# A two-branch attention kernel on one core: another order of the units, the last output rows in halves, the first weights in column halves

## The chip, the core and the metric

The kernel runs on one core of a Trainium2 chip. A core has a matrix engine (TensorE, PE in the profile), a vector engine (VectorE, DVE), a scalar engine (ScalarE, ACT), a general engine (GpSimd, POOL) and a queue engine (SyncE, SP) that here issues every DMA. Each engine runs its own instructions in order and waits on semaphores for the others. Matmuls write to eight banks of an accumulation memory (PSUM); ACT and DVE copy results out of it ("evacuate" it). The metric is the device time of one execution in microseconds (us), the median of the runs.

## The reference, cut to what matters

Two branches read the same x of 2048 rows by 512 and are mixed row by row with a gate. Everything is bf16.

```python
# branch A: 64 segments of 32 rows, 32 heads of 128, one after the other
mem = mem0                                   # 8 rows
for s in range(64):
    h = concat([mem, x[32*s : 32*s + 32]])   # 40 rows
    q, k, v = h @ Wq, h @ Wk, h @ Wv         # 512 -> 32 x 128 each
    p = softmax(where(mask, q @ k.T * scale, -1e9))
    o = (p @ v) @ Wo
    mem = o[:8]                              # the next segment reads it
    outs.append(o[8:])
# branch B: 4 blocks of 512 rows, 32 heads of 16
for s in range(4):
    a_dot = softmax(qs @ ks.T * scale + causal) @ vs
    a_mem = (phi(qs) @ M) / (phi(qs) @ z + 1e-6)      # M, z sum phi(k).T @ v over earlier blocks
    o_B = sigmoid(beta) * a_mem + (1 - sigmoid(beta)) * a_dot
b = concat(o_B) @ wo
g = sigmoid((x * gate_w).sum(-1))
out = g * a + (1 - g) * b
```

Segment s+1 of branch A needs the 8 memory rows that segment s puts out, so the segments form a chain. Branch B is free of it and fills gaps.

## The kernel before

**First phase (to about 50 us).** x, branch B's weights and then branch A's weights (4 MB each for Wk, Wq, Wv) are loaded. x is turned by TensorE (`x_chunk`, L588), and `b_projections` works out K, Q and V of branch B for three of the four blocks. `pk` (L686) multiplies one quarter f (128 of the 512 columns) of wk or wq with a block's x; its result is evacuated to `stgk[f]` and stored to DRAM (`scr_kqd`). `pv` (L704) does the same for V, `mz` (L738) for the memory matrix `MZ` (stored to `scr_mzd`). `plan_loads` issues the loads, in this order: x of block 0, wk, wq, wv of branch B, x of block 1, small things, x of blocks 2 and 3, the gate's weights. Tiles of this phase share their memory with tiles of the second one, so a tile's first use there waits for the last use here.

**Second phase (from 50 us).** `plan_a` runs 16 lists of unit names, `A_LIST0` to `A_LIST15`, one for each group of four segments. A unit adds its instructions to the queues of its engines in the order of the list. Nothing else orders the work, so a list sets what each engine does next, and an instruction that isn't ready holds back all that is queued behind it on its engine. The names, for segment r (0 to 3) of the group and head half b:

- `r.Kbx`, `r.Kby` (also Q, V): the two halves of a projection on TensorE (L1291, 8 matmuls each); `r.kb`, `r.qb`, `r.vb`: its evacuation; `r.TKb`, `r.TQb`: the turn of it on DVE (L1303).
- `r.Sb` scores (L1571, L1576), `r.Xb` exponential, `r.Yb` mask, `r.Mb` sums (L1606), `r.Lb` reciprocal as logarithm and exponential on ACT (L1613, L1616), `r.Nb` normalisation on DVE (L1620), `r.nb` that of the left rows on POOL (L1626).
- `r.PVb`, `r.PLb`: P times V and its left part (L1636, L1648); `r.E..`: evacuation; `r.W..`: output projection in four parts (L1378); `r.Hb`: evacuation to `WF`; `r.Fb`: fold, a small matmul that brings the four row groups together (L1396); `r.hmb`: the memory rows for the next segment; `r.axb`: the output rows to `aT_st`.
- `KL..`, `QL..`, `VL..`: projections of the last 8 rows of each of a group's segments, which the next step gives as "left" rows (with `i` ahead of the name for group 0, and `e` behind it for the evacuation); `VLt` loads the left V back from `scr_vld`; `ol..`, `of` and `ofe`: their output projection, fold and evacuation (`pl..`, `pf` for the last group). `xl`, `xc`, `qt`, `oL`: copies on POOL.
- `bS`, `bE`, `bP`, `bT`: the next scores (L919), exponential (L940, masked on POOL, L946), PV (L972) and finishing step of branch B; `pj`, `pp`: a half projection of B's fourth block (L823) and its evacuation; `wl`: the next 512 KB of Wo.
- `os`: the turn of a finished group's output rows (L1453) and their four stores to `scr_aTd` (L1457); `tl`: the load of the next group's rows into the one tile `aTg` (L1476); `tb`, `tbe`: B's output rows of the group, `brow` (L1487), and their scaling by 1 − g to `t1_sb` (L1495); `tf`, `tfe`: the final sum `fin` (L1520) and the store of the result (L1522).
- `~` behind a name swaps ACT and DVE for its evacuation.

The last group's rows don't go through DRAM: `f_atr` (L1511) turns them on TensorE from `aT_st`. In the kernel before, that group's tail units come after the end of list 15, in the loop at the end of `plan_a`: `brow`, one `t1`, `f_atr` into one bank, then `fin` and the store in two halves of 256 columns.

Of the kernel before, what the change touches and what calls it, by code (L numbers as in the profile page):

```python
# [257 lines left out]
def build(nc, es, A_x, A_mem0, A_Wq, A_Wk, A_Wv, A_Wo, B_wq, B_wk, B_wv, B_wo, B_beta, gate_w, out, dbg=None):  # L258
    v = NS()
# [108 lines left out]
    def over(home):  # L368
# [3 lines left out]
        for p in v.under[home]:  # L372
            p = parts.get(p, p)
            for n, r in list(R.items()):
                if n == p or p in ("V17", "phK") and n.startswith(p) or p.startswith("stgk") and n[:-1] == p:
                    ops += ([r.w] if r.w else []) + r.readers
# [138 lines left out]
def plan_loads(v, A_x, A_mem0, A_Wq, A_Wk, A_Wv, B_wq, B_wk, B_wv, B_wo, B_beta, gate_w):  # L515
# [11 lines left out]
    for nm, dst, src in (("wk", v.wkB, B_wk), ("wq", v.wqB, B_wq), ("wv", v.wvB, B_wv)):  # L527
        ld("b" + nm, dst[:, :, :].rearrange("p (h n) m -> p h (n m)", h=2), src.rearrange("(h p n) m -> p h (n m)", h=2, n=2), nm + "B", "dma_" + nm)
# [120 lines left out]
def b_projections(v):  # L649
# [29 lines left out]
    def pk(sb, f, m):  # L679
# [8 lines left out]
        P.op("pe", fp, reads=x_res(v, sb) + [Rs(wr)], writes=[v.rbank[bk]], name="p%s%d_%d" % (m, sb, f))  # L688
# [166 lines left out]
class BAttn:  # L855
# [205 lines left out]
    0.K0x 0.Q0x bE bE 0.Q0y 0.K0y 0.q0~ 0.TQ0 xl 0.k0 0.TK0 0.Q1x 0.K1x 0.Q1y 0.q1 bP bP 0.qt bT 0.K1y 0.k1 0.TK1 0.V1x 0.S0 0.X0 0.TQ1 0.V1y bS VL0x 0.Y0
# [199 lines left out]
def plan_a(v, nseg):  # L1261
# [206 lines left out]
    def tail_units(g):  # L1468
# [6 lines left out]
        if not last:  # L1475
            P.dma(P.group("al%d" % g, "al"), lambda sp: sp.dma_start(aTg[:, :, :].rearrange("p c t -> p (c t)"), v.aTd[g]), reads=[Rs("aTd%d" % g)], writes=[Rs("aTg")],  # L1476
                  name="lda%d" % g, scratch=True)

        def ub():
            bb = B.take()  # L1480

            def f_(pe):
                ins = None
# [376 lines left out]
```

## Time and profile before

| | |
|---|---|
| median of 3 runs | 842.63 us (841.31 to 843.46) |
| the profiled execution | 841.9 us, of which the span from the first to the last instruction is 839.7 us |
| granted TensorE clock | 1.000 |
| PE busy | 806.0 us, 96% of the span |
| ACT, DVE, POOL busy | 590.3, 576.5, 286.1 us |
| moved by DMA | 57.48 MB |

The times of the lines shown come from this one execution. A line of the timeline gives start, duration, engine, source line, operation, output tile <- input tiles, form and count, and in brackets the idle time of the engine before it and what ended it. "PE ps L686" in a wait means the matmul of line 686. SPq lines are DMA issues on SP's queue: their duration is that of the issue, not of the transfer. `A_x` is loaded into the memory of `Wo_sb`, `wvB` is `woB_sb`, and `t_sb` is `t1_sb`.

### The profile page before, as it was taken

What the parts mean: (1) busy time and instruction counts of PE and PEld (TensorE: products, weight loads), DVE (VectorE), ACT (ScalarE), POOL (GpSimd) and SP (SyncE); (2) the same over time, 40 slices, a digit from 0 to 9 for tenths busy, and PEclk for the clock granted to TensorE, in tenths of its full rate; (3) what the DMA queues carried; (4) which work ended last, traced back from release to release, by engine and by line L of the source; (5) the groups of instructions that cost most, each with busy time, mean ns of one, the idle gap of its engine ahead of it and who ended that gap; (6) DMA issues with size and microseconds to landing.
All of it is one profiled execution on the core that took longest, in us unless ns stands there. A gap on an engine that the chain in (4) does not pass through costs nothing.

```text
span 839.7 us, 49011 instructions
## 1 busy us (share of the span) xinstructions
PE 806.0 (96%) x21927; PEld 431.3 (51%) x21933; DVE 576.5 (69%) x1395; ACT 590.3 (70%) x1506; POOL 286.1 (34%) x780
## 2 busy tenths in 40 slices
PE   8988999999999999999999999999999999999997
PEld 4644455555555555554555555555555555555443
DVE  4554566677576767766767767867688777777764
ACT  5546777677777777776787676777766676777554
POOL 3613233333333333334343333334233333333210
PEclk9999999999999999999999999999999999999999
DMA  9997212112111111111111021211102021110111
GB/s 324 418 360 228 67 45 60 48 31 54 25 30 40 31 44 34 44 38 46 25 44 39 24 56 25 47 38 46 37 19 55 22 55 26 47 35 16 29 41 46
DMA packets 98225, 57.48 MB, mean 68 GB/s; under 512 B 71768, under 2 KB 92128, under 8 KB 96480
## 3 DMA queue, kind: packets, MB, share of 16 engines
q1 hardware_dynamic: 98016, 54.36, 22.2%
q8 instruction: 172, 2.82, 1.4%
q14 instruction: 37, 0.30, 0.1%
HBM read 37.14 MB, written 17.20 MB: 65 GB/s over the span
## 4 chain that ended last, share of the span: by engine, by line
PE 84%; ACT 6%; DMA 4%; DVE 3%; issue 1%; SPq 1%; DVEq 0%; ACTq 0%
PE ps L1291 45%; PE ps L1378 17%; PE ps L1396 3%; PE ps L1636 3%; PE ps L919 2%; PE ps L686 2%; PE ps L972 2%; DMA scr_mzd<-MZ 2%; PE ps L1571 2%; PE ps L1487 1%; PE ps L1606 1%; ACT PT L940 1%; ACT R_sb L1616 1%; ACT WF L390 1%; PE ps L704 1%
## 5 line engine op out<-in xcount | busy, mean ns | idle before, releaser
L946 POOL TENSOR_SCALAR_AFFINE_SELECT PT<-PT 128x128 bf16<-128x128 bf16 (+2 forms) x320 | 118.1, 369 | 202.4 <-ACT PT L940 155.5
L940 ACT ACTIVATE PT<-ps 128x512 bf16<-128x512 f32 x320 | 175.1, 610 | 5.7 <-PE ps L919 4.6
L1291 PE MATMUL ps<-Wv_sb,hT 128*32 128x512 bf16 x2048 | 138.4, 379 | 0.0
L1291 PE MATMUL ps<-Wq_sb,hT 128*32 128x512 bf16 x2048 | 136.7, 379 | 0.7
L1291 PE MATMUL ps<-Wk_sb,hT 128*32 128x512 bf16 x2048 | 135.9, 379 | 1.4 <-ACT PT L940 1.1
L1378 PE MATMUL ps<-Wo_sb,OT_sb 128*32 128x512 bf16 x2048 | 129.2, 380 | 0.7 <-ACT OT_sb L390 0.6
L1626 POOL TENSOR_TENSOR P_sb<-P_sb,R_sb 128x64 bf16<-128x64 bf16 x128 | 51.0, 398 | 135.6 <-ACT R_sb L1616 129.4
L390 ACT ACTIVATE OT_sb<-ps 128x320 bf16<-128x320 f32 x170 | 68.7, 435 | 23.4 <-PE ps L1648 21.9
L1291 PEld LDWEIGHTS ps<-Wk_sb,hT 128*32 128x32 bf16 x2048 | 58.0, 97 | 47.6 <-ACT hT L390 2.1
L1291 PEld LDWEIGHTS ps<-Wq_sb,hT 128*32 128x32 bf16 x2048 | 57.7, 97 | 48.0 <-ACT hT L390 3.6
L390 ACT ACTIVATE WF<-ps 128x256 f32<-128x256 f32 x105 | 35.2, 382 | 55.2 <-PE ps L1378 53.0
L1378 PEld LDWEIGHTS ps<-Wo_sb,OT_sb 128*32 128x32 bf16 x2048 | 47.9, 96 | 45.4 <-ACT OT_sb L390 7.3
L1303 DVE STREAM_TRANSPOSE QT_sb<-QN_sb 128x256 f32<-128x256 f32 x128 | 56.3, 440 | 21.6 <-ACT QN_sb L390 18.0
L390 ACT ACTIVATE QN_sb<-ps 128x512 bf16<-128x512 f32 x78 | 46.9, 604 | 34.3 <-PE ps L1291 32.8
L1303 DVE STREAM_TRANSPOSE KT_sb<-KN_sb 128x256 f32<-128x256 f32 x128 | 56.3, 440 | 20.8 <-ACT KN_sb L390 17.7
L390 ACT ACTIVATE KN_sb<-ps 128x512 bf16<-128x512 f32 x75 | 45.1, 602 | 31.8 <-PE ps L1291 31.1
L1585 ACT ACTIVATE P_sb<-ps 128x224 bf16<-128x224 f32 x128 | 45.9, 360 | 28.4 <-PE ps L1576 20.3
L1291 PEld LDWEIGHTS ps<-Wv_sb,hT 128*32 128x32 bf16 x2048 | 50.1, 95 | 24.3 <-ACT aT_st L390 0.6
L1620 DVE TENSOR_TENSOR P_sb<-P_sb,R_sb 128x160 bf16<-128x160 bf16 x128 | 42.2, 330 | 20.2 <-ACT R_sb L1616 18.2
L392 DVE CAST V_sb<-ps 128x512 bf16<-128x512 f32 x76 | 51.8, 682 | 5.4 <-PE ps L1291 4.8
L392 DVE CAST OT_sb<-ps 128x320 bf16<-128x320 f32 x86 | 41.1, 486 | 19.0 <-PE ps L1648 18.1
L1636 PEld LDWEIGHTS ps<-P_sb,V_sb 32*128 32x128 bf16 x2048 | 23.3, 91 | 59.7 <-DVE P_sb L1620 25.2
(139 smaller groups left out, 1483.0 us busy)
## 6 DMA issues: line engine op xcount, KB each, us to landing
Wk_sb<-in_A_Wk_dram SPq DMA_DIRECT2D x4, 1024.0 KB, 9.8
Wq_sb<-in_A_Wq_dram SPq DMA_DIRECT2D x4, 1024.0 KB, 13.3
Wv_sb<-in_A_Wv_dram SPq DMA_DIRECT2D x4, 1024.0 KB, 15.3
Wo_sb<-in_A_Wo_dram SPq DMA_DIRECT2D x8, 512.0 KB, 5.8
scr_vld<-VNL SPq DMA_DIRECT2D x16, 256.0 KB, 2.1
VL<-scr_vld SPq DMA_DIRECT2D x64, 64.0 KB, 2.7
scr_kqd<-stgk SPq DMA_DIRECT2D x12, 256.0 KB, 9.5
Vj<-scr_vd SPq DMA_DIRECT2D x32, 68.0 KB, 2.4
```

The lines of the kernel that those rows point to most:

```text
L390: P.op("act", lambda a: a.activation(dst, src, ACT.Copy), reads=[v.rbank[k] for k in bks], writes=dres, name=name)
L392: P.op("dve", lambda d: d.tensor_copy(dst, src), reads=[v.rbank[k] for k in bks], writes=dres, name=name)
L940: P.op("act", lambda a: a.activation(pt, v.pb[bk], ACT.Exp, scale=v.SCALE_B), reads=[v.rbank[bk]], writes=[rp], name="be%d_%d" % (n, t))
L946: P.op("gp", lambda g: g.affine_select(mv, mv, [[0, len(cut)], [1, 128]], ALU.is_ge, 0.0, base=0, channel_multiplier=-1), reads=[rp], writ ...
L1291: ins = pe.matmul(pb[bk][SEG * j:SEG * (j + 1), :], lhs(c), cols(w, j) if split else w[:, 512 * j:512 * (j + 1)], start=(c == 0), stop=(c ...
L1303: P.op("dve", lambda d: d.transpose(to, src), reads=reads, writes=writes, name=name)
L1378: ins = pe.matmul(pb[bk][SEG * j:SEG * (j + 1), :], lhs(4 * k + j), Wo_sb[:, 4 * k + j, :], start=(first and k == ks[0]), stop=False, skip ...
L1396: ins = pe.matmul(pb[bk][SEG * j:SEG * (j + 1), SEG * n:SEG * (n + 1)], cols, v.fold[:, :], start=True, stop=True, skip_group_check=True)
L1585: P.op("act", lambda a: a.activation(P_sb[:, b, :], pb[bk][:, 0:224], ACT.Exp, scale=SCALE), reads=[rbank[bk]], writes=[Rs("P%d" % b), Rs( ...
L1620: P.op("dve", lambda d: d.tensor_tensor(wide(P_sb, b)[:, :, 0:L], wide(P_sb, b)[:, :, 0:L], R_sb[:, b, :].rearrange("p (i q) -> p i q", q= ...
L1626: P.op(ENG["n"], lambda d: d.tensor_tensor(left(P_sb), left(P_sb), grp04(R_sb[:, b, :]), ALU.mult), reads=[Rs("R%d" % b)], writes=[Rs("P%d ...
L1636: ins = pe.matmul(pb[bks[j]][:, L * i:L * (i + 1)], V_sb[SEG * j:SEG * (j + 1), b, i * E:(i + 1) * E], P_sb[SEG * j:SEG * (j + 1), b, LW * ...
```

## The change

Three things change together.

1. The loads of B's wk and wq go by halves of their columns: first columns 0 to 255 of wk and of wq, then 256 to 511, each half in two DMAs (two of the four row blocks each). A quarter f of a projection waits for its half alone. All other loads keep their order behind these.
2. All 16 lists are new. Of some 270 to 360 units in each, 14 to 54 stand at the same place as before. The work is the same: only fillers (`bE`, `bP`, `bT`, `os`, `tl`, `tf`), which do nothing when there is nothing to do, differ in number. In list 15, `ofe os` (the turn and the stores of group 14) stand in segment 1 of the group instead of `os` in segment 2, and `tl tb` of the last group stand ahead of `3.F0`.
3. The last group's tail is done in halves of 256 columns: `brow` as two sets of 16 matmuls into two banks, with the first half's scaling right behind the first set; `f_atr` as two sets of 8 matmuls into two banks, each waiting for one half of the last segment's rows (`aTe0`, `aTe1`); each half of `fin` waits for its halves alone. The last group's tail may be loaded before its rows are done.

The diff, cut to its core (lists: the first lines of list 0 and the last lines of list 15):

```diff
     x(0)
-    for nm, dst, src in (("wk", v.wkB, B_wk), ("wq", v.wqB, B_wq), ("wv", v.wvB, B_wv)):
-        ld("b" + nm, dst[:, :, :].rearrange("p (h n) m -> p h (n m)", h=2), src.rearrange("(h p n) m -> p h (n m)", h=2, n=2), nm + "B", "dma_" + nm)
+    for half in range(2):
+        for nm, dst, src in (("wk", v.wkB, B_wk), ("wq", v.wqB, B_wq)):
+            m = slice(256 * half, 256 * half + 256)
+            for h in range(2):
+                ld("b%s%d" % (nm, half), dst[:, 2 * h:2 * h + 2, m], src.rearrange("(h p n) m -> h p n m", h=2, n=2)[h][:, :, m],
+                   "%sB%d" % (nm, half), "dma_%sp%d%d" % (nm, half, h))
+    ld("bwv", v.wvB[:, :, :].rearrange("p (h n) m -> p h (n m)", h=2), B_wv.rearrange("(h p n) m -> p h (n m)", h=2, n=2), "wvB", "dma_wv")
     x(1)
...
-        P.op("pe", fp, reads=x_res(v, sb) + [Rs(wr)], writes=[v.rbank[bk]], name="p%s%d_%d" % (m, sb, f))
+        P.op("pe", fp, reads=x_res(v, sb) + [Rs("%s%d" % (wr, f // 2))], writes=[v.rbank[bk]], name="p%s%d_%d" % (m, sb, f))
...
 A_LIST0 = """
-    ixl iKL0x iQL0x iQL0 iQL1x iQL1 iKL0 pj iKL1x iKL0e iKL1 wl 0.Q1x 0.Q1y iQL1e pj 0.K0x 0.K0y 0.q1 0.TQ1 iQL0e~ iKL1e~ bS wl bE iVL0x 0.V0x bE 0.V0y bE
-    0.xc bE 0.Q0x 0.v0~ pp 0.Q0y 0.q0 0.TQ0 bS bP wl bP 0.qt 0.k0~ 0.TK0 pj bE pj wl bE 0.S0 0.X0 iVL0 iVL1x iVL1 0.K1x wl 0.K1y iVL0e~ bE 0.Y0 0.M0 pj xl
-    pp 0.k1 iVL1e wl wl iVLt bE 0.L0 0.TK1 bP wl 0.S1 0.X1 bS 0.Y1 bP bE bE pj bE KL0x 0.M1 0.n0 bE 0.L1 pp 0.V1x 0.V1y 1.xc QL0x 0.v1 QL0 QL0e~ QL1x QL1
+    wl ixl iQL0x iKL0x 0.Q1x 0.Q1y iKL0 iKL0e~ wl iQL0 iQL0e~ 0.Q0x 0.Q0y iQL1x iQL1 0.K0x 0.K0y 0.k0 iQL1e pj 0.q1 wl iKL1x iKL1 iKL1e~ bS bE 0.V0x 0.q0
+    iVL0x 0.TQ0 0.V0y 0.V1x pj 0.V1y iVL0 0.TK0 pj pp 0.v1 bE 0.qt bE iVL0e~ pj bE iVL1x iVL1 xl bS iVL1e bP 0.xc bP QL0x bE bE 0.TQ1 0.v0 0.S0 wl 0.K1x
+    0.K1y KL1x bE wl 0.X0 0.Y0 bE KL1 pj pp 0.k1~ KL1e wl iVLt wl 0.TK1 0.M0 0.L0 QL0 bP wl QL0e bS 0.N0 bP bE VL0x VL0 0.S1 1.qt bE 0.X1 bE QL1x 0.Y1
...
 A_LIST15 = """
...
-    tf 2.F0 2.hm0 2.ax0 pl0 2.F1 2.hm1 3.K0x 3.Q1x 3.K0y 3.Q0x tfe 3.Q0y 3.K1x 3.K1y 3.k0 tl 3.Q1y 3.TK0 3.q0 3.TQ0 3.k1 3.TK1 pl1x 3.S0 3.V0x 3.q1 3.V0y
-    3.X0 3.TQ1 3.S1 3.X1 2.ax1 3.Y0 3.M0 3.Y1 3.L0 3.n0 tb 3.v0 tbe 3.N0 tf 3.V1x 3.M1 tfe 3.PV0 3.PL0 3.L1 3.n1 3.N1 3.V1y 3.E0b~ 3.E0a 3.v1~ pl1 3.W0a
-    3.PV1 3.PL1 pl1e 3.W0b pf 3.E1b~ pfe 3.E1a 3.W1b 3.W1a 3.H0 3.H1 tb 3.F0 3.ax0~ tbe 3.F1 3.ax1 tf tfe
+    2.H0 2.H1 2.F0 2.hm0 pl0 2.F1 2.hm1 3.K0x tfe 3.Q0x 2.ax0~ 3.Q0y 3.q0~ 3.K0y 3.k0 3.TQ0 3.K1x 3.K1y 3.Q1x tl 3.Q1y 3.TK0 3.S0 3.V0x 3.k1~ 3.q1 3.TK1
+    3.X0 3.TQ1 pl1x 3.V0y 3.Y0 3.S1 3.M0 2.ax1 3.X1 tb 3.v0 3.Y1 3.L0 3.n0 tbe 3.V1x 3.M1 tf 3.N0 tfe 3.L1 3.n1 3.N1 3.PV0 3.PL0 3.E0b~ 3.E0a 3.V1y 3.v1~
+    pl1 pl1e 3.W0a 3.PV1 3.PL1 3.W0b pf 3.E1b~ 3.W1b 3.E1a pfe~ 3.W1a 3.H0 3.H1 tl tb 3.F0 3.ax0 3.F1 3.ax1 tbe tf tfe
     """
...
-        rr = [Rs("aTl%d" % (g % 2))] + [Rs("aTx%d_%d" % (g % 2, r)) for r in range(4)] if last else [Rs("aTg")]
+        rr = [Rs("aTl%d" % (g % 2))] + [Rs("aTx%d_%d" % (g % 2, r)) for r in range(3)]
...
+        n = 2 if last else 1
         def ub():
-            bb = B.take()
...
+            bbs = [B.take() for _ in range(n)]
+            def brow(h):
+                def f_(pe):
+                    ins = None
+                    for f in range(C):
+                        for j in range(4):
+                            q = slice(SEG * j, SEG * (j + 1))
+                            c = slice(512 // n * h, 512 // n * (h + 1))
+                            ins = pe.matmul(pb[bbs[h]][q, c], oTg[:, f, q], woB_sb[:, f, c], start=(f == 0), stop=(f == C - 1))
+                    return ins
+                P.op("pe", f_, reads=[Rs("oTg"), Rs("woB")], writes=[rbank[bbs[h]]], name="brow%s%d_%d" % ("h" if last else "", g, h))
+            brow(0)
+            if last:
+                t_rows(0, bbs[0])
             if g % 4 < 3:
                 b_rows(g + 1)
-            return lambda: ub2(bb)
+            return lambda: ub2(bbs, brow)
...
+        def ub2(bbs, brow):
+            if last:
+                brow(1)
+            t_rows(n - 1, bbs[n - 1])
+            B.give(*bbs)
...
+            for h in range(n):
+                def f_atr(pe, h=h):
+                    ins = None
+                    for c in range(h * C // n, (h + 1) * C // n):
...
+                P.op("pe", f_atr, reads=rr + [Rs("aTe%d" % h), Rs("ident")], writes=[rbank[bks[h]]], name="atrh%d_%d" % (g, h))
...
-                evac(("act", "dve")[hf], dst[:, hf], folded(wb["f%d" % hf]), [wb["f%d" % hf]], [Rs("aTx%d_%d" % (par, r)), Rs("aTl%d" % par)], "atx%d_%d" % (s, hf))
+                evac(("act", "dve")[hf], dst[:, hf], folded(wb["f%d" % hf]), [wb["f%d" % hf]], [Rs("aTe%d" % hf)], "atx%d_%d" % (s, hf))
...
-        if t < ngrp and len(stored) > t and bat.jobs_done >= 4 * (t // 4) + 4 and "tb" not in units and "tf" not in units and "tf" not in pend:
+        if t < ngrp and (t == ngrp - 1 or len(stored) > t) and bat.jobs_done >= 4 * (t // 4) + 4 and "tb" not in units and "tf" not in units and "tf" not in pend:
```

More of the change, by code (lines that the diff above doesn't have):

```diff
@@ L374, in over @@
             for n, r in list(R.items()):
-                if n == p or p in ("V17", "phK") and n.startswith(p) or p.startswith("stgk") and n[:-1] == p:
+                if n == p or p in ("V17", "phK", "wkB", "wqB") and n.startswith(p) or p.startswith("stgk") and n[:-1] == p:
                     ops += ([r.w] if r.w else []) + r.readers
@@ L1059 @@
+    3.oL 3.F1 3.hm1~ 3.ax1
     """
 A_LIST1 = """
[L1061 to L1063 removed]
```

391 lines of the change are left out of this document (188 added, 203 removed).

## The prediction

> **What bounds the kernel now.** I read the page's busy times first, then the slices, the waits in the stretch where the DMA engines are full, and the timeline of the end.
>
> ```profile
> PE 806.0 (96%) x21927; PEld 431.3 (51%) x21933; DVE 576.5 (69%) x1395; ACT 590.3 (70%) x1506; POOL 286.1 (34%) x780
> ...
> PEclk9999999999999999999999999999999999999999
> DMA  9997212112111111111111021211102021110111
> ```
>
> TensorE (PE) sets the time at full granted clock, and the change leaves its matmul work as it is (I count 2,255 TensorE units in the old lists and in the new). So only gaps between units can be won or lost. A busy share of 96% hides them, since ends of matmuls are modelled. I therefore took start-to-start times from the timeline: a projection half-pass (8 matmuls of 512 columns) never follows the one before in under 0.43 us, a PV block takes 0.105, a fold 0.123, B scores 0.327. Summed so, the units from the first list unit (50.58 us) to the last fold (834.66) need 704.3 us; they took 784.1. The 79.7 us of gaps stand 30.5 before PV (128 of them, 0.238 each), 13.0 before folds, 11.1 before B scores (0.11 each even when nothing is late), 7.6 before K and Q projections, 4.1 before the left PV, 3.3 before B's PV. By place: 9.3 in 50 to 100 us, 6.3 in 800 to 835, and 3.7 to 5.8 in each 50 us between.
>
> DMA is full in the first three slices of 21 us (9, 9, 9, then 7), and this is what that does before the lists begin, in the waits from 30 to 57 us:
>
> ```profile
> DVE MZ L744 <- DMA scr_mzd<-MZ: 3.9, 1, 3.9
> ACT stgk L390 <- DMA scr_kqd<-stgk: 3.3, 2, 2.5
> DVE stgk L392 <- DMA scr_kqd<-stgk: 2.7, 2, 1.4
> ```
>
> Evacuations of branch B's third block wait for stores of the second that sit behind megabytes of weights. Those landings, not TensorE, pace 38 to 50 us.
>
> The end, timeline:
>
> ```profile
> 821.88 3.03 SPq L1457 DMA_DIRECT2D scr_aTd<-aT_st  x4
> ...
> 824.96 0.60 SPq L1522 DMA_DIRECT2D out_dram<-aTg  x1
> ...
> 826.94 0.33 SPq L1476 DMA_DIRECT2D aTg<-scr_aTd  x1
> ...
> 830.48 0.75 DVE L1520 SCALAR_TENSOR_TENSOR aTg<-aTg,g_sb,t_sb 128x512 bf16<-128x512 bf16 x1 [1.76 <-ACT V_sb L390]
> 831.15 0.32 DVE L1620 TENSOR_TENSOR P_sb<-P_sb,R_sb 128x160 bf16<-128x160 bf16 x1
> ...
> 831.61 0.28 PE L1636 MATMUL ps<-P_sb,V_sb 32*128 32x40 bf16 x16 [1.01 <-DVE P_sb L1620]
> ...
> 834.39 0.61 PE L1396 MATMUL ps<-fold,WF 128*32 128x32 f32 x32 [0.47 <-ACT WF L390]
> ...
> 835.93 0.69 ACT L1495 ACTIVATE t_sb<-ps,omg_sb 128x512 f32<-128x512 f32 x1 [1.32 <-PE ps L1487]
> 836.70 0.88 DVE L1520 SCALAR_TENSOR_TENSOR aTg<-ps,g_sb,t_sb 128x256 bf16<-128x256 f32 x2 [1.35 <-ACT t_sb L1495]
> ```
>
> The reader sees a chain through SyncE's (SP) queue: four stores of group 14 take 3.03 us, group 13's output waits behind them to 824.96, the load of group 14's rows waits for that output to leave the shared tile, lands near 830.4, and only then can VectorE (DVE) finish group 14 (830.48) and do the normalisation queued behind it (831.15), for which the last PV waits. After the last fold come, one after the other, B's output row, its scaling (0.69), two halves of the final sum (0.88), and the store.
>
> **First weights in column halves.** Two 512 KB loads become eight of 128 KB. Each issue took 0.47 us on SP (wkB 1.80 to 2.27), so six more hold wv, x1, beta, mem0, x2, x3, gw and the first store back by about 2.9 us. What lay queued covers it: gw's issue ended at 8.99 and it landed at 14.87, so 2.9 us later the queue still holds work. The first K matmul waits less: it started at 7.58, waiting for all of wkB; the x tiles are turned by 6.58. Half the bytes should be there by then, so TensorE starts 0.95 us earlier, and the 0.21 wait for wqB goes too: up to −1.1. It doesn't last. The stgk and MZ evacuations above are released by landings at 38.9, 42.0, 45.1 and 52.6, and nothing in an earlier start brings those forward. They come later if anything: rows of 256 columns make 512-byte packets. In the trace's packet records those take 27 ns against 84 for 2,048 bytes, so 1 MB in them costs 2,048 x 27 / 16 = 3.5 us instead of 2.7, +0.8 on a full queue. Bounds −1.1 and +0.8; I take +0.4, nearer the row that gates (the landings).
> The Trainium skill speaks for and against this edit. "DMA: Bandwidth & Descriptors", Specifications, puts line rate at 512 bytes and up; by it the term would be 0, and the packet records disagree by a quarter (19 bytes per ns against 24). "Perfetto Trace Analysis", DMA Optimizations, says that splitting DMAs may help if the DMA engines are generally idle; slices of 9 say that here they aren't. Taken as if they were idle, the term would be −1.1 and the sum 1.5 lower.
>
> **The new order, list 0** (50.58 us to the first fold at 80.62). 23.6 us of work took 30.0: 6.45 of gaps. The largest: B scores 0.97 and 0.31, B's PV 0.65 and 1.20, the left PV 1.06 (waiting for the load of VL), the fold 0.72. In the new list B's first PV stands 5.1 us of TensorE work behind its scores instead of 2.5, which covers its four exponentials (2.07 us) and masks. V's left evacuation comes after three Wo loads instead of five, so its store has 1 MB less ahead of it and the load of VL behind it lands earlier. Against it: V's first evacuation moves from ScalarE (ACT) to DVE, and it waits there for the last mzd store (60.7); B's left V, a Q transpose and the other V queue behind it. I take −2.0: 0.65 + 1.06 and a quarter of the 1.2. Bounds −4 (two thirds of the gaps) and +1.5 (the DVE queue stands still for two more evacuations of 0.69).
>
> **The new order, lists 0 to 15.** For each consumer I added the TensorE work listed between its producer and itself, in both lists, and gave the new list the mean gap that the old trace shows for that distance. For PV behind its softmax sums (us of cover: count before, count after, mean gap before):
> 0.15–0.5: 6, 4, 0.77; 0.5–0.7: 5, 7, 0.50; 0.7–0.9: 4, 1, 0.37; 0.9–1.1: 18, 20, 0.37; 1.1–1.3: 13, 13, 0.11; 1.3–1.6: 46, 47, 0.18; 1.6–2: 25, 24, 0.15; over 2: 11, 12, 0.14.
> That gives 29.8 against 30.5: −0.7. The same sum gives folds −0.2, K and Q −0.7, B's PV −0.6 (those directly behind their last exponential fall from 6 to 3), output projections +0.3. Together −1.9; some of it lies in list 0 and the end, so −1.5 here. The cover says nothing of the queues of ACT and DVE: 50 us stretches scatter by 0.5 around 4.6, and if all 14 went to the better or worse side that is ±7. I use −6 and +5.
>
> **The end.** Group 14's fold and turn move from segment 62 to segment 61, so its four stores leave SP some 11 us earlier; on SP they are moved past the load of group 14's B rows alone, which then stands 3 us behind them and isn't needed for a segment; on DVE the transpose (0.43) is moved past a segment's evacuations. Group 13's output then issues at about 822.6, the load at 824.6, landing at 828, and group 14's final sum runs when its scaled row is there (828.7), before the normalisation is due. The last PV's gap of 1.19 falls to the usual 0.1: −1.1. Then the halves: the first half of B's last row (16 matmuls of 256 columns, 0.43) goes ahead of the fold, where TensorE sat for 0.66 waiting for the evacuation of WF, so it is free; if that cover were gone it would cost its 0.43. Counted from the end of the last output projection (833.73): ACT does two WF halves (to +0.93), the first scaled half (0.38 by the 128x256 row, to +1.35), the first row evacuation (+1.58), the second scaled half (+2.15); the final sums end at +2.9 instead of 837.58 − 833.73 = 3.85. −0.95. Splitting adds a wait of ACT's second scaling on a matmul, and behind that nothing is queued but the end. Sum −2.0; bounds −2.6 and 0 (the load still late, and the row evacuation held up behind the scaling).
>
> **Sum.** The profiled execution took 841.9 (span 839.7 and 2.2 around it): 841.9 + 0.4 − 2.0 − 1.5 − 2.0 = 836.8. The median of the three runs, 842.63, is 0.7 above it, so the forecast is 837.5.
>
> **Rivals.** (1) Only the end pays: list 0's stalls are DMA landings in any order, the start costs its 0.8, the rest evens out: 842.6 − 2.0 + 0.8 = 841.4, no change. For it: the cover tables are nearly alike. Against it: the left PV's wait follows from the place of Wo loads, which does change. (2) Slower: ACT becomes the queue that PV waits for. The swap marks move 16 evacuations from DVE to ACT (I count 1,456 ACT operations in the lists before, 1,472 after): at 0.44 each, 7.0 us on the engine that already is the busier (70% against 69%) and that does both steps of the reciprocal before each PV. If that adds 0.08 us to each of 128 gaps, +10: 837.5 + 10.2 = 847.7. It decides from a mean gap of 0.30 (0.238 + 7.6/128), where the whole gain and 2.5 more are gone. Against it: between sums and their reciprocal stand 0.72 other ACT operations on average, 0.87 before. (3) The halves don't do what they say: the scaled half delays the row evacuation as much as it saves, and group 14's load stays late: no gain at the end, 839.5.
>
> **Numbers.** About 0.3% (2.5 us: below 840.1, above 845.2) is what a measurement of this kernel can tell from no change. Forecast 0.57; rival 1 0.16; rival 2 0.17; rival 3 0.10, still just faster. So faster 0.67, same 0.16, slower 0.17. The range reaches down by the bounds of list 0 and the order to 832, and up past rival 1 into rival 2, to 846.
>
> **What would show it.** Right: the first K matmul near 6.6 us, yet the first list unit still at 50.5 to 51.5; the left PV of segment 0 without a DMA wait; the mean gap before PV at 0.22 to 0.24; the last PV without 1.0 us of waiting; the final sums ending 2.9 us after the last output projection. Wrong: gaps of over 5 us in most 50 us stretches, DVE standing for the mzd store while B scores wait, or the first list unit moving by over 1 us either way.

## The result: 0.5% faster, and the profile after

The changed kernel took 838.72 us (median of 13 runs, 838.09 to 841.79), the kernel before on the same chip 842.88 us (13 runs): ratio 0.9953, 95% interval 0.9939 to 0.9966. The forecast was 837.5 us.

The profiled execution of the new kernel is one of its longest (841.79 us, span 840.0, against 841.9 and 839.7 before), so its trace can't be laid beside that of before as a whole. It has to be read by stretch. Of its page, the busy times and two of the 40-slice rows:

```profile
PE 809.5 (96%) x21949; PEld 435.9 (52%) x21949; DVE 571.8 (68%) x1379; ACT 597.2 (71%) x1523; POOL 283.9 (34%) x780
...
PEclk9999999999999999999999999999999999999999
DMA  8998211211101111111101121211112111110121
```

ScalarE (ACT) has 6.9 us more, as the 16 moved evacuations were to give. DMA shows 8, 9, 9, 8 where it showed 9, 9, 9, 7: the same bytes, later. The waits from 30 to 57 us (engine and line waited, what for: total us, times, longest):

```profile
ACT stgk L390 <- DMA scr_kqd<-stgk: 6.8, 3, 3.0
DVE stgk L392 <- DMA scr_kqd<-stgk: 5.2, 3, 2.3
...
PE ps L725 <- DVE stgk L392: 2.6, 2, 2.0
DVE MZ L749 <- DMA scr_mzd<-MZ: 2.3, 1, 2.3
```

The two waits for stores of stgk grew from 3.3 and 2.7 us, and one of them now reaches TensorE (2.6). The end, timeline:

```profile
814.02 0.32 SPq L1481 DMA_DIRECT2D aTg<-scr_aTd  x1
...
814.39 3.30 SPq L1462 DMA_DIRECT2D scr_aTd<-aT_st  x4
...
823.56 0.34 SPq L1540 DMA_DIRECT2D out_dram<-aTg  x1
...
825.28 0.33 SPq L1481 DMA_DIRECT2D aTg<-scr_aTd  x1
...
831.66 0.75 DVE L1537 SCALAR_TENSOR_TENSOR aTg<-aTg,g_sb,t_sb 128x512 bf16<-128x512 bf16 x1 [0.34 <-ACT t_sb L1508]
...
833.11 0.27 PE L1654 MATMUL ps<-P_sb,V_sb 32*128 32x40 bf16 x16
...
835.68 0.61 PE L1401 MATMUL ps<-fold,WF 128*32 128x32 f32 x32
835.79 0.48 ACT L1508 ACTIVATE t_sb<-ps,omg_sb 128x256 f32<-128x256 f32 x1
...
836.99 0.88 DVE L1537 SCALAR_TENSOR_TENSOR aTg<-ps,g_sb,t_sb 128x256 bf16<-128x256 f32 x2 [0.39 <-PE ps L1529]
```

Group 14's four stores are issued by 817.69, 5.9 us before group 13's output, the load of group 14's rows leaves 6.4 us ahead of the final sum that reads it, and that sum now waits for its scaled row alone. The last PV doesn't wait for the normalisation any more; its weight load stood 0.42 us for an evacuation of V on ScalarE. The last sums end at 837.87, 2.85 us after the last output projection (835.02).

The start-to-start method of the prediction, applied to each stretch between the same TensorE units of all the profiled executions (us; columns: first list unit; from there to the first fold of segment 3; on to that of segment 59; to that of 61; to the last PV; to the last fold; to the span's end):

| kernel | first unit | to seg. 3 | 3 to 59 | 59 to 61 | to last PV | to last fold | rest | half clock |
|---|---|---|---|---|---|---|---|---|
| before | 50.58 | 65.48 | 671.70 | 22.13 | 21.72 | 2.77 | 5.31 | none |
| after | 53.09 | 66.79 | 670.69 | 22.27 | 20.26 | 2.56 | 4.32 | 85.24 |
| after_again | 53.92 | 63.05 | 671.64 | 22.26 | 20.26 | 2.56 | 4.31 | 44.02 |
| order_only | 51.96 | 66.68 | 670.61 | 22.32 | 20.26 | 2.56 | 5.31 | 8.60, 83.70 |
| halves_only | 52.62 | 65.36 | 672.13 | 22.13 | 20.87 | 2.77 | 5.33 | none |
| whole_first | 51.90 | 63.33 | 670.38 | 22.25 | 20.27 | 2.56 | 4.31 | none |
| tail_only | 50.65 | 67.20 | 674.16 | 22.13 | 21.49 | 2.77 | 4.30 | 63.74 |
| os_late | 51.03 | 64.86 | 670.71 | 22.28 | 20.26 | 2.56 | 4.30 | none |
| pp_later | 51.96 | 63.91 | 671.64 | 22.28 | 20.26 | 2.56 | 4.29 | 8.14 |
| rows_split | 53.30 | 62.63 | 670.90 | 22.25 | 20.27 | 2.56 | 4.30 | 10.66 |
| os_later | 50.78 | 65.81 | 670.98 | 22.31 | 20.26 | 2.57 | 4.30 | none |
| weights_later | 50.78 | 68.55 | 670.13 | 22.28 | 20.26 | 2.56 | 4.32 | 62.29 |
| small_late | 50.55 | 65.94 | 670.70 | 22.25 | 20.27 | 2.56 | 4.33 | 77.73 |
| os_h1 | 50.66 | 66.87 | 671.51 | 22.25 | 21.65 | 2.77 | 4.29 | 82.58 |

The spans are known to 0.1 us, and the stretch that ends with them no better. The last column is where a stretch of 3.41 us at half granted clock begins (those behind the last matmuls are left out). Between before and after it reads: +2.51 at the first unit, +1.31 in the first segments, −1.01 in the middle, +0.14, −1.46, −0.21 and −0.99 at the end, together +0.3 (840.0 − 839.7). So the gain that these two traces show lies in the middle and at the end, and the profiled execution lost it again in the first 120 us. The two traces understate the difference: this execution took 3.1 us more than its kernel's median, and the profiled one of the kernel before 2.2 us less than the median of 23 later runs (844.07); where a usual run of the kernel before spends those 2.2 us no trace shows.

### The profile page after: what moved, and what is told of

Same layout as the page of the kernel before. It is cut to its first block, busy times and chain, and to the rows that moved or that the text cites. A ratio compares the mean times of both kernels' runs of the same rounds, so it can differ in the third digit from the quotient of the medians.

```text
span 840.0 us, 49042 instructions
## 1 busy us (share of the span) xinstructions
PE 809.5 (96%) x21949; PEld 435.9 (52%) x21949; DVE 571.8 (68%) x1379; ACT 597.2 (71%) x1523; POOL 283.9 (34%) x780
## 4 chain that ended last, share of the span: by engine, by line
PE 82%; ACT 8%; DVE 4%; DMA 4%; issue 2%; SPq 1%; POOL 0%; DVEq 0%; ACTq 0%
PE ps L1296 44%; PE ps L1383 16%; PE ps L1401 3%; PE ps L1654 3%; PE ps L924 2%; PE ps L977 2%; DMA scr_kqd<-stgk 2%; PE ps L691 2%; PE ps L1589 1%; PE ps L1496 1%; PE ps L1624 1%; ACT PT L945 1%; ACT R_sb L1634 1%; ACT WF L390 1%; DVE P_sb L1638 1%
## 5 line engine op out<-in xcount | busy, mean ns | idle before, releaser
L1296 PE MATMUL ps<-Wq_sb,hT 128*32 128x512 bf16 x2048 | 139.2, 382 | 0.4
L1644 POOL TENSOR_TENSOR P_sb<-P_sb,R_sb 128x64 bf16<-128x64 bf16 x128 | 50.5, 395 | 146.1 <-ACT R_sb L1634 137.7
L390 ACT ACTIVATE OT_sb<-ps 128x320 bf16<-128x320 f32 x167 | 67.0, 434 | 24.3 <-PE ps L1666 22.8
L390 ACT ACTIVATE QN_sb<-ps 128x512 bf16<-128x512 f32 x85 | 51.0, 600 | 31.2 <-PE ps L1296 29.8
L390 ACT ACTIVATE KN_sb<-ps 128x512 bf16<-128x512 f32 x82 | 49.3, 602 | 27.8 <-PE ps L1296 27.3
```

The lines of the kernel that those rows point to most:

```text
L390: P.op("act", lambda a: a.activation(dst, src, ACT.Copy), reads=[v.rbank[k] for k in bks], writes=dres, name=name)
L1296: ins = pe.matmul(pb[bk][SEG * j:SEG * (j + 1), :], lhs(c), cols(w, j) if split else w[:, 512 * j:512 * (j + 1)], start=(c == 0), stop=(c ...
L1644: P.op(ENG["n"], lambda d: d.tensor_tensor(left(P_sb), left(P_sb), grp04(R_sb[:, b, :]), ALU.mult), reads=[Rs("R%d" % b)], writes=[Rs("P%d ...
```

## The experiments

Ratios are to the kernel before in runs on the same chip. Its median there was 844.07 us beside after_again, order_only, whole_first and halves_only, 843.44 beside tail_only, os_late, pp_later and rows_split, 844.34 beside os_later, small_late and weights_later, and 844.04 beside os_h1.

**The new kernel once more.**

> The changed kernel once more, for a second profile. In the first one it took 841.8 us, 3.1 over its median of 838.7: between 82 and 84 us TensorE stood for 2.0 us (a store of branch B's fourth block landed late and held ACT), and from 85.2 to 88.7 us the granted clock was at half. Theory 1 (the stall is a chance of that execution): 838.7, no stretch at half clock, the first fold within 31 us of the first list unit. Rival (it is always there): the same 2.0 us gap and half clock, and a profiled time of 841 to 842.

838.96 us (6 runs), ratio 0.9945 [0.9924, 0.9966]; profiled 839.81. The stall at the first fold is shorter (0.7 us against 2.0), and a stall from 40.6 to 42.6 us was followed by half clock instead: the theory holds for the one stall, and not for the absence of half clock.

**The new lists alone** (`A_LIST0` to `A_LIST15` of after in the kernel before; loads and last rows as before).

> The kernel before with the 16 new lists alone: loads whole, last rows as before. Theory 1 (the column halves of the first weights cost 2.5 us, because the first list unit moved from 50.6 to 53.1 us, and the halves of the last rows give 1.0): 842.9 - 5.2 = 837.7. Rival (the halves of the first weights cost nothing, the later start belongs to that one execution): the order gives only 4.2 - 1.0 = 3.2, so 839.7.

839.29 us (12 runs), ratio 0.9949 [0.9933, 0.9966]: −4.8 us, within its noise the whole gain, and nearer the first theory's −5.2 than the rival's −3.2. The end of the table shows the parts: last PV 20.26 as in after, the rest 5.31 as before.

**The new kernel with whole first weights.**

```diff
-    for half in range(2):
-        for nm, dst, src in (("wk", v.wkB, B_wk), ("wq", v.wqB, B_wq)):
-            ...
+    for nm, dst, src in (("wk", v.wkB, B_wk), ("wq", v.wqB, B_wq), ("wv", v.wvB, B_wv)):
+        ld("b" + nm, ...)
```

> The changed kernel with the first weights loaded whole again; order and halves of the last rows stay. Theory 1: 838.7 - 2.5 = 836.2, first list unit at 50.6 us. Rival (nothing): 838.7. Second rival, the edit's own promise that TensorE starts 1.1 earlier and keeps it: 839.8.

837.42 us (6 runs), ratio 0.9934 [0.9911, 0.9957]. It is the fastest median of all, 1.5 us under the unchanged new kernel on the same chip, though the two intervals overlap. Its first list unit came at 51.90 us, not at the 50.6 that the theory named.

**The column halves alone** (the diff above the other way round, in the kernel before).

> The kernel before with the first weights in column halves alone. Theory 1: 842.9 + 2.5 = 845.4, first K matmul at 6.6 us instead of 7.6, first list unit at 53.1. Rival: 842.9. Second rival (the start is kept): 841.8.

844.09 us (12 runs), ratio 1.0004 [0.9988, 1.0020]: 0.3 us with −1.0 to +1.7. The 2.5 us of the first theory aren't there, and the rival's gain of 1.1 isn't either. The first K matmul did start at 6.75 us, but the first list unit came at 52.62 instead of 50.58.

**The last rows alone.**

```diff
-    ... 3.W1a 3.H0 3.H1 tb 3.F0 3.ax0~ tbe 3.F1 3.ax1 tf tfe
+    ... 3.W1a 3.H0 3.H1 tl tb 3.F0 3.ax0~ 3.F1 3.ax1 tbe tf tfe
```

> The kernel before with its own lists and whole weights, and only the last output rows of both branches worked out in halves (the load of the last rows, tl, is put ahead of tb at the end of list 15). My theory, that this part pays by itself and that its size is read at the end: the stretch from the last fold to the end of the span falls from 5.31 to 4.3 us, the stretch from the first fold of segment 61 to the last PV stays at 21.7 us, and the time is 1.0 us below the kernel before (843.1 where that one is 844.1). Rival: the halves pay only together with the earlier store of group 14, since group 14's final sum still stands in front of the end on VectorE; then the last stretch is 5.0 us or more and the time is that of before (843.8 to 844.4).

843.03 us (12 runs), ratio 0.9993 [0.9977, 1.0009]. The time can't tell −1.0 from 0; the stretch can: 4.30 us from the last fold to the end, against 5.31, with the last PV still late. The theory is right on size and place. This execution also names the wait that the prediction had only argued:

```profile
831.74 0.33 SPq L1476 DMA_DIRECT2D aTg<-scr_aTd  x1
...
834.50 0.75 DVE L1532 SCALAR_TENSOR_TENSOR aTg<-aTg,g_sb,t_sb 128x512 bf16<-128x512 bf16 x1 [1.53 <-DMA aTg<-scr_aTd]
835.16 0.32 DVE L1633 TENSOR_TENSOR P_sb<-P_sb,R_sb 128x160 bf16<-128x160 bf16 x1
```

The load of group 14's rows landed 2.7 us after its issue, at 834.4, and the normalisation for the last PV stood behind the sum. (In the timeline of before the same idle time was put down to an evacuation of V on ScalarE. That evacuation ended at 830.38, and the load landed then too, 3.4 us after its issue at 826.94.)

**Group 14's stores later** (in whole_first, two attempts that came to one program).

```diff
-    ... 1.W1b 1.W1a of ofe os 1.H0 ...      2.H0 2.H1 2.F0 2.hm0 pl0 ...
+    ... 1.W1b 1.W1a of ofe 1.H0 ...         2.H0 2.H1 os 2.F0 2.hm0 pl0 ...      (os_late)
+    ... 1.W1b 1.W1a of ofe 1.H0 ...         2.H0 2.H1 2.F0 2.hm0 pl0 os ...      (os_later)
```

> The new kernel with whole first weights (837.4 us), with one mark moved: the four stores of group 14 (os) leave SyncE in segment 62 behind the second half of its output projection, about where they stood before, and not in segment 61. My theory, the chain through SyncE's queue: group 13's output row and the load of group 14's rows stand behind the stores again, the last PV waits for VectorE by about 1 us, the stretch from the first fold of segment 61 to the last PV goes from 20.27 back to 21.4 to 21.8 us, and the time rises by 1.2 us to 838.6. Rival: the order of the other units around it is what gained, and the stores may stand where they like: the stretch stays at 20.3 us and the time at 837.4.

> The new kernel with whole first weights, with the four stores of group 14 (os) moved further back than in os_late: behind the fold of segment 62, so that they leave SyncE about 12 us after the first fold of segment 61 (in the kernel before 11.99, in os_late 9.75, in the new order 2.2). My theory, that the chain through SyncE's queue exists but that os_late left it 1 us of slack: group 13's output now stands behind the stores (3 us), the load of group 14's rows leaves at about 17 us after that fold, the last PV waits for VectorE again, and the stretch from that fold to the last PV goes from 20.27 to 21.2 us or more; the time rises by 1.0 to 1.5 us over the whole-weights kernel (837.4 to 838.0 so far). Rival: what gained is that group 13's final sum comes 2 us sooner (9.9 us after that fold instead of 11.9) and the place of the stores is worth nothing: the stretch stays at 20.3.

837.81 us (five runs, 836.62 to 839.98; a sixth, of 1985.05, is left out of the comparison), ratio 0.9926 [0.9899, 0.9953]; os_later, the same order on every engine, 838.75 us (6 runs), 0.9930 [0.9906, 0.9954]. The stretch stayed at 20.26 in both, so on the face of it the rival wins. But the stores left only 9.75 us after the fold of segment 61, and the timeline of os_late shows a chain with little slack left:

```profile
818.63 2.68 SPq L1457 DMA_DIRECT2D scr_aTd<-aT_st  x4
...
821.36 0.60 SPq L1535 DMA_DIRECT2D out_dram<-aTg  x1
824.90 0.33 SPq L1476 DMA_DIRECT2D aTg<-scr_aTd  x1
...
827.69 0.75 DVE L1532 SCALAR_TENSOR_TENSOR aTg<-aTg,g_sb,t_sb 128x512 bf16<-128x512 bf16 x1 [0.34 <-ACT t_sb L1503]
```

That load landed 2.1 us after its issue, at 827.0; the scaled row was ready at 827.66, and the sum began at 827.69. So some 0.7 us of slack were left. A further step was wanted, and moving the mark alone had not given it: the transpose behind it runs on VectorE (DVE), where the next order is set by other instructions.

> The new kernel with whole first weights, with os behind the second output projection of segment 62 and that projection's second evacuation given to VectorE (2.H1~ os), as the kernel before had it. The move in os_later changed the order of no engine against os_late, so it ran the same program; here the transpose of group 14 does come behind VectorE's half of WF, as in the kernel before, while group 13's final sum keeps its earlier place in the list. In os_late the load of group 14's rows landed just as the scaled row was there (18.8 us after the first fold of segment 61). My theory, the chain through SyncE's queue: stores at 11.5 to 12 us after that fold instead of 9.75, group 13's output behind them at 14.5 to 15, the load at 16.8 to 17.6 instead of 16.0, landing 2.8 us later at 19.6 to 20.4, so that the final sum of group 14 and the last PV wait for it: the stretch to the last PV 21.0 to 21.7 us against 20.27, and the time 0.8 to 1.4 us above os_late (838.0 and 838.75). Rival: the load still lands by 18.8 us, since group 13's output isn't held up; the stretch stays at 20.3 and the time at 838.

```diff
-    ... 2.H0 2.H1 2.F0 2.hm0 pl0 ...
+    ... 2.H0 2.H1~ os 2.F0 2.hm0 pl0 ...
```

```profile
822.40 0.42 DVE L392 COPY WF<-ps 128x256 f32<-128x256 f32 x1 [1.74 <-ACT WF L390]
822.74 0.43 DVE L1453 STREAM_TRANSPOSE aT_st<-aT_st 128x256 f32<-128x256 f32 x1
823.10 0.71 DVE L1532 SCALAR_TENSOR_TENSOR aTg<-aTg,g_sb,t_sb 128x512 bf16<-128x512 bf16 x1
823.20 3.10 SPq L1457 DMA_DIRECT2D scr_aTd<-aT_st  x4
826.35 0.60 SPq L1535 DMA_DIRECT2D out_dram<-aTg  x1
828.33 0.33 SPq L1476 DMA_DIRECT2D aTg<-scr_aTd  x1
...
831.80 0.75 DVE L1532 SCALAR_TENSOR_TENSOR aTg<-aTg,g_sb,t_sb 128x512 bf16<-128x512 bf16 x1 [2.05 <-DMA aTg<-scr_aTd]
```

Here the chain of before is back link by link, and the stretch is 21.65 us, +1.38 on whole_first; 839.69 us (6 runs), ratio 0.9945 [0.9926, 0.9964], 0.9 to 1.9 above os_later and os_late (which ran on other chips; the intervals overlap). Counted from the fold of segment 61 the load left 1.0 us later than in os_late, and it took 3.4 us to land instead of 2.1; why it took longer was not tried. The theory holds in the trace, and it gets a finer form: what made the chain late in the kernel before was VectorE's half of WF (`2.H1~`), which waits 1.74 us for ScalarE with the transpose and group 13's sum queued behind it.

**ScalarE's wait in list 0.** In the profiled new kernel the largest gap of list 0 is a new one:

```profile
82.59 0.62 ACT L390 ACTIVATE t_sb<-ps 128x512 bf16<-128x512 f32 x1 [2.60 <-DMA scr_vd<-t_sb]
83.10 0.37 ACT L390 ACTIVATE WF<-ps 128x256 f32<-128x256 f32 x1
...
83.53 0.33 PE L1401 MATMUL ps<-fold,WF 128*32 128x32 f32 x16 [2.04 <-ACT WF L390]
```

The mark `pp`, which evacuates branch B's late V into a tile that a store still reads, stands ahead of the first fold's evacuation in the new list 0.

```diff
-    0.W1a bP pp bT 0.W1b 0.H0 0.H1~ ... 0.F1 0.hm1~ 1.K0x
+    0.W1a bP bT 0.W1b 0.H0 0.H1~ ... 0.F1 0.hm1~ pp 1.K0x
```

> The new kernel with whole first weights, with one mark moved in list 0: pp, the evacuation of branch B's late V block by ScalarE into a tile that a store still reads, goes from ahead of the second evacuation of WF of segment 0 to behind the first segment's mean (0.hm1). Theory: ScalarE's wait for that store (1.8 us with whole weights, 2.6 in the new kernel) stands ahead of the first fold no more. The gap before the first fold falls from 1.2 us to 0.3 or less and the first fold comes 0.8 to 1.1 us sooner after the first left PV (pv0_0 to wf0_0 5.3 to 5.6 us against 6.41); the time falls by 0.8 to 836.6, and there is no stretch of half granted clock behind 80 us. Rival: the store that this evacuation feeds then lands later, and branch B's late V block holds up the next of its steps: the first fold of segment 3 comes no sooner (115.2 us) and the time stays at 837.4 or above.

838.11 us (6 runs), ratio 0.9933 [0.9907, 0.9960]. The wait for the store is gone, and TensorE's idle time before the first fold fell from 1.21 to 0.67 us (now for VectorE's half of WF). But from the first PV to the first fold it still took 6.33 us against 6.41, since the output projection ahead of it ended 0.5 us later; most of that is the left PV, which stood 1.17 us in this execution and 0.82 in whole_first. The time shows no gain over whole_first; the rival's number fits, and its mechanism (a later step held up) wasn't seen. What the move is worth stays open.

**Eight issues of whole rows.**

```diff
+    for q in range(4):
+        for nm, dst, src in (("wk", v.wkB, B_wk), ("wq", v.wqB, B_wq)):
+            h, p = q // 2, slice(64 * (q % 2), 64 * (q % 2) + 64)
+            ld(..., dst[p, 2 * h:2 * h + 2, :]..., src...[h][p, :], ...)
```

> The new kernel with the first two weights again in eight loads of 128 KB, but each of whole rows (64 partitions with 2,048 bytes each) in place of 256 columns of 128 partitions (512 bytes each); TensorE waits for the whole of a weight. It tells apart what makes the start slower in the new kernel (first list unit 53.1 and 53.9 us, against 51.9 with two whole loads). Theory: the number of issues on SyncE, 0.47 us each, starves the DMA engines early; then this kernel is as slow at the start as the new one: bytes moved from 0 to 20 us about 1 MB under the kernel before (266 against 318 GB/s), first list unit at 53 to 54 us, time 838.7. Rival: the 512-byte packets cost it; then the rate from 0 to 20 us is near 318 GB/s, the first list unit at 52 us and the time at 837.4.

840.57 us (12 runs), ratio 0.9954 [0.9936, 0.9972]. The windows from 4 to 20 us, for the new kernel, rows_split and whole_first in that order (last three columns: granted clock, DMA share, GB/s):

```profile
4.00:8.00 4.00, 3.15 (x21) 2.06 (x19) 0.76 (x2) 1.09 (x2) 1.92 (x4) 1.00 0.78 213
8.00:12.00 4.00, 4.00 (x23) 1.97 (x22) 1.92 (x4) 1.53 (x3) 0.00 (x0) 1.00 0.97 280
12.00:20.00 8.00, 8.00 (x60) 4.46 (x58) 5.48 (x13) 6.46 (x13) 2.48 (x13) 1.00 0.95 345
```

```profile
4.00:8.00 4.00, 2.99 (x20) 1.95 (x17) 0.76 (x2) 1.09 (x2) 1.93 (x4) 1.00 0.82 223
8.00:12.00 4.00, 2.71 (x9) 0.97 (x10) 0.69 (x1) 0.07 (x1) 0.00 (x0) 0.83 0.89 289
12.00:20.00 8.00, 8.00 (x54) 4.40 (x53) 4.60 (x10) 5.17 (x11) 0.00 (x0) 0.87 0.97 353
```

```profile
4.00:8.00 4.00, 1.88 (x21) 1.21 (x19) 0.75 (x2) 1.08 (x2) 1.93 (x4) 1.00 0.87 260
8.00:12.00 4.00, 3.54 (x20) 1.58 (x19) 1.38 (x2) 1.12 (x2) 0.00 (x0) 1.00 0.98 338
12.00:20.00 8.00, 7.95 (x59) 4.46 (x59) 5.86 (x14) 6.29 (x14) 2.03 (x10) 1.00 1.02 377
```

With packets of 2,048 bytes the eight issues start as slowly as with packets of 512. So it is the issuing on SyncE (SP): one load of 128 KB left every 0.64 us, 131 KB / 0.64 us = 205 GB/s, half of what the 16 DMA engines moved in a full slice of the page (416 in the new kernel, 418 in the kernel before). Over the page's first slice (21 us) the four kernels with eight issues moved 268 to 279 GB/s, and the eight with two (before, tail_only, order_only, whole_first, pp_later and the three with later stores) 301 to 324. The middles, 274 and 311, differ by 0.8 MB in 21 us, and at 418 GB/s that is 1.9 us, close to what the first list unit lost (halves_only +2.0). The first list unit came at 53.30, as the theory had it. The time did not: it is 1.9 us above the theory's 838.7. This execution ran at half clock from 10.66 us on, and all 12 runs had a granted clock below 1 (0.994 to 0.998). "DMA: Bandwidth & Descriptors" of the Trainium skill, Specifications, puts line rate at 512 bytes and up. No run here tests that: by the packet records of the prediction 512-byte packets could move 16 × 512 / 27 = 303 GB/s, an estimate above the 205 that the issuing let through.

**The small loads moved, and the weights of branch A spread.** In whole_first, beta and mem0 behind x2 and x3; and, separately, one of the twelve loads of branch A's weights (1 MB each) at every fourth piece of branch B's projections instead of every third.

```diff
-    x(1); beta; mem0; x(2); x(3)
+    x(1); x(2); x(3); beta; mem0                     (small_late)
-        if weights and n % 3 == 2:
+        if weights and n % 4 == 3:                   (weights_later)
```

> The new kernel with whole first weights, with the two small loads beta and mem0 (0.94 and 0.60 us on SyncE for a few KB) moved behind the third and fourth block of x. It takes 1.5 us of SyncE's issuing from ahead of x2 and x3, the reverse of the six extra issues that the column halves bring. Theory, that the issuing on SyncE starves the DMA engines in the first 10 us: the rate from 0 to 21 us rises from 301 to 316 GB/s to 325 or more, the first list unit comes 0.3 to 0.6 us sooner than 51.0 to 52.0, and the time falls by about 0.4 us. Rival: while these two are issued the queue still holds more than 1 MB (2.5 MB issued, about 1 MB moved by 5 us), so it never runs dry: rate, first unit and time stay (301 to 316 GB/s, 51 to 52 us, 837.4 to 838.0).

> The new kernel with whole first weights, with the twelve 128 KB-row loads of branch A's K, Q and V weights issued every fourth piece of branch B's projections instead of every third, so that fewer of them stand ahead of B's stores. Theory, that these stores behind weights pace 38 to 50 us: ScalarE's and VectorE's waits for the stores of stgk between 30 and 57 us fall from 8.5 us in sum (5.0 and 3.5) to 6 or less, branch B's last piece ends 1 us sooner or more, and if the later weights are still in time the first left units come sooner and the time falls by about 1 us to 836.5. Rival: all bytes up to 75 us are needed by then and the DMA engines are full, so what the stores gain, branch A's projections lose: the first left unit or the first V waits for a weight, the first fold comes at 80.5 to 81.5 us as before, and the time stays at 837.4 to 838.0.

small_late: 838.00 us (8 runs), ratio 0.9935 [0.9912, 0.9958]. Its first slice had 322 GB/s, against 300 to 316 in the whole-weights kernels of the new order and 325 or more asked by the theory, and its first list unit came at 50.55, 0.1 to 1.4 us ahead of theirs. One execution can't tell that from their scatter, and the time didn't follow: the rival's number.

weights_later: 844.16 us (12 runs, 837.51 to 850.03), ratio 1.0001 [0.9974, 1.0029]: the waits go as the theory had it, and the time is a loss. The waits for stores of stgk between 30 and 57 us went from 8.5 us to none. But the first list unit came at 50.78, no sooner than in the other kernels with two issues (50.55 to 51.96), and then

```profile
PE ps L1291 <- DMA Wv_sb<-in_A_Wv_dram: 4.9, 1, 4.9
```

the first V projection stood for the last weight, and a half-clock stretch followed. In the other thirteen executions of the table the first list unit followed the landing of the eighth store of stgk by 5.5 to 5.9 us (45.1 and 50.58 in the kernel before, 47.6 and 53.09 in the new one). So the landings do pace 38 to 50 us, as the prediction had it. Here that store landed at 39.3, and the first list unit waited for something else: to free the landings was worth nothing while the same DMA engines owed list 0 its weights.

## Why the prediction was right, and where it was not

**The end (−2.0): right, both halves of it.** The last PV came 1.46 us sooner than in the profiled kernel before (forecast 1.1), with the chain through SyncE as its cause (os_h1). How much it is differs by execution: the other two with the old lists took 20.87 and 21.49 us for that stretch, 0.6 and 1.2 more than the new one, and in all three the last PV came 1.1 us after the sum that waits for the load. The last rows in halves gave 0.99 (forecast 0.95), alone and with the rest.

**The order in lists 0 to 15 (−1.5): right in sum, not in its parts.** From segment 3 to 59 the three kernels with the old lists took 671.70, 672.13 and 674.16 us, the eleven with the new ones 670.13 to 671.64, middle 670.71: −1.0 on the profiled before, −1.4 on the middle of the three. The two sets only just don't overlap. The cover tables were to explain it, and did not in size: gaps before PV fell by 2 to 3 us (by how the unit ahead is charged) and not 0.7, those before B's PV by 1.8 and not 0.6, those before K and Q together by 1.6 (whole_first) and 0.2 (after) against 0.7, and those before folds rose by 1.1 and 1.9 where they were to fall by 0.2. No run separates what else moved PV. Rival 2 is out: the mean gap before PV is 0.215 to 0.22, at the lower edge of the 0.22 to 0.24 forecast and far from 0.30.

**First weights in halves (+0.4, bounds −1.1 and +0.8): the step that failed.** "What lay queued covers it": it didn't. DMA moved 1.0 MB less by 20 us than in the kernel before (windows: 71 × 4 + 76 × 4 + 56 × 8 = 1,036 KB), and the first list unit came at 53.09, outside the 50.5 to 51.5 that the prediction named, and by more than the 1 us that it had set as a sign of being wrong. The way there is the one that the prediction had named as the gate: the stores of stgk landed later by the same 2.5 us. The term at that unit is near +2 (52.62, 53.09, 53.92 and 53.30 with eight issues, against 50.6 to 52.0 with two), above the upper bound, and it comes from issues, not packets (rows_split). How much of it reaches the end is open: 0.3 us in the kernel before and 1.5 on the same chip in the new one, both with intervals that hold 0. Two of the new-order kernels that start late take 63.05 and 62.63 us from there to segment 3, as if part of the time was waited out anyway. "Perfetto Trace Analysis" in the Trainium skill, DMA Optimizations, says that a split may help if the DMA engines are generally idle. They weren't (DMA shares of 0.78 to 0.97 from 4 to 20 us), and the −1.1 for that case didn't come. The first K matmul in the new kernel started at 7.78, not 6.6: x was turned at half clock there (1.85 us, full clock granted from 6.73 on), and in halves_only, without that, at 6.75 as forecast.

**List 0 (−2.0): the stretch is shorter, but hardly anything of it is gained.** In the six new-order executions without a half-clock stretch between the first unit and segment 3 it took 62.63 to 65.81 us, middle 63.6, against 65.48 and 65.36: −1.8. But the shortest two are those with a late first unit, and with whole weights the new list's first unit also comes later (50.66 to 51.96, against 50.58 and 50.65; why was not tried). The four of the six with whole weights reached the first fold of segment 3 at 115.23 to 116.59 us, middle 115.9, and the kernel before at 116.06: −0.2 where −2.0 was forecast. B's PV lost its gaps as forecast. The left PV's wait for the load of VL did not go (1.0 us in after, 1.4 in after_again). And `pp` ahead of the first fold was missed: TensorE's idle time before it went from 0.55 us to 2.04 in the new kernel, 0.7 in after_again and 1.21 in whole_first.

**The sum.** Rival 1 (only the end pays) is out in its number by order_only, though its account of list 0, landings in any order, fits the traces better than the forecast's. Rival 3 is out by the end's stretches. The forecast started from one execution (841.9) and added 0.7; beside the new kernel the kernel before measured 842.88. Of the 1.2 us by which 838.72 misses 837.5, 0.3 are this base, and 0.9 that the difference is −4.2 and not −5.1 (after_again, on its chip, had −5.1). That the sum came so near is in part luck. Up to segment 3 the forecast had a gain of 1.6 us, and against the kernel before after_again was there 0.9 us later and whole_first 0.8 sooner. What makes up for it seems to be that usual runs of the kernel before are slower than its profiled one; no trace shows where.

## What to carry to other kernels

A chain that ends in one late load is best priced by each link's slack: in os_late the stores could go 7.5 us later for nothing, with 0.7 us of slack left, and in os_h1 the next 2.2 us cost 1.4. Before splitting a load, divide the bytes of a piece by the time of its issue and compare that with the rate of the DMA engines: here it was 205 against 418 GB/s, and the split cost 2 us at the first list unit. Where the first stretch of a kernel is full of transfers, freeing one wait can hand its time to the next one that the same engines owe, as in weights_later.

## What the hardware showed that was not expected

Half clock after short stalls. Each of the stretches in the table is 3.41 us long, and they begin on a grid of 3.41 us counted from the moment at which full clock was first granted (in after 85.24 = 6.73 + 23 × 3.413). The windows of the new kernel around one:

```profile
80.00:85.00 5.00, 2.75 (x92) 1.64 (x87) 2.06 (x5) 2.41 (x7) 0.80 (x2) 1.00 0.42 121
85.00:90.00 5.00, 5.00 (x77) 3.13 (x69) 2.51 (x5) 1.69 (x4) 1.22 (x3) 0.66 0.41 91
```

In the 3.41 us ahead of all ten, TensorE was busy for 0.00 to 1.82 us; where it was busy for 1.9 of a grid step or more it kept its clock, and between 1.5 and 1.8 both were seen. So phase decides: after and after_again had the same stall on stgk, here in this order.

```profile
42.26 0.40 PE L725 MATMUL ps<-ident,stgk 128*128 128x128 bf16 x4 [2.02 <-DVE stgk L392]
42.64 0.40 PE L725 MATMUL ps<-ident,stgk 128*128 128x128 bf16 x4 [2.03 <-DVE stgk L392]
```

In after it straddled a grid line at 40.86 and cost nothing more; in after_again it lay within one step (from 40.60 on) and was followed by half clock. By estimate a stretch costs up to 3.41 / 2 = 1.7 us. Part of the scatter of 3 to 4 us between executions of one kernel goes with it, by the granted clock on record for each run. In order_only the four runs at 1.000 took 838.56 us on average and the five at 0.998 took 840.38; in weights_later the one run at 1.000 took 837.51, and the two with the lowest clock (0.991 and 0.992) 847.94 and 848.35. Of the new kernel's 13 runs it explains nothing: three at 1.000 averaged 839.42, nine at 0.998 839.05. "TensorE: Matmul & The Clock Gate" of the Trainium skill, Part 1, describes the free-running window of 3,413 ns, and the traces agree with that. Its rule that gaps over about 3.4 us are what to avoid is too lenient here: in nine of the ten cases the longest gap was 0.8 to 2.3 us.
